# Top-k attention and a mixture of experts on one core: eight small routing operations per loop step for the first three batches, nine for the choices made on incomplete counts

## The chip, the core and the metric

The kernel runs on one core of a Trainium2 chip. The metric is the device time of one execution in microseconds (us), the median of several executions. Five engines work side by side, each through its own queue of instructions in program order: PE (TensorE, matmuls), DVE (VectorE), ACT (ScalarE), POOL (GpSimd) and SP (SyncE, which issues transfers here). They wait for each other through semaphores.

## What is computed

Inputs are q, k and v (8 batches, 8 heads, 576 positions, 64 columns), a modality per token, a gate of 8 experts and the experts' weights. Per head, every row of scores keeps its 32 largest values, and the softmax over them weighs v. The 4608 rows of 512 columns go to the expert with the largest logit:

```
scores = scale * np.matmul(q, k.transpose(0, 1, 3, 2))
kth = np.partition(scores, -top_k, axis=-1)[..., -top_k:-top_k + 1]
scores = np.where(scores >= kth, scores, -1000000000.0)
attn = softmax(scores)
x = np.matmul(attn, v), rows of all heads side by side
logits = x @ w_gate + modality_bias[modality_id]
e_idx = np.argmax(logits, axis=1)
out[e_idx == e] = gate_w * (np.maximum(x @ w1[e], 0.0) @ w2[e])
```

## The kernel before

**The attention loop.** The 32 pairs of heads are cut into 9 tiles of 128 rows each, 288 tiles in all, 36 to a batch. The loop over `i` takes one step per tile and works on many tiles at once, each at another stage. In step `i` PE makes the scores of tile i + 2 (L396), ACT copies them to `Ssb` (L404), and DVE finds the eight largest of each of seven pieces of tile i (`subs`, L411, "piece maxima"). For tile i - 1 DVE runs the selection chain (`chain`, L422 to L424: MAX8, MATCH_REPLACE8 and so on, each reading what the one before wrote). ACT makes `K` (L443), POOL the product `y` (L449), DVE the MAX8 over `y` (L453, `find`), every third step three operations that pick the threshold (`pick`, L460 to L462), ACT the exponential `ex` (L467), and DVE ends the step with `keep` (L473), which writes the masked probabilities `P`. POOL waits for `P` (`gate`, L477) before it makes the next `y`. PE transposes `P` (L488) and multiplies with v (L516).

**The order on DVE within a step.** It is written out by hand. List `a_` is the chain, `b_` the piece maxima and `find`, and `c_` the pick, the small operations of the step and `keep`. If `c_` holds more than `keep`, up to HOLD = 4 entries of `b_` are held back and put between the last entries of `c_`. `weave` spreads the rest of `b_` behind the entries of `a_`.

**Routing.** When a batch is done, `logits`, `logit_rows` and `xrow` bring its rows and logits into place, and `route` returns a list of small operations: bias, maximum, exponential (ACT, `r_ez`, L631), one-hot (L632 to L635), `ranks` (PE L607 to L611, ACT copy `r_rk`, L612), two products on POOL (L640, L641, put in `behind`, which is run at the step's end), the sum of the gate (L642 to L644), `total` (L616, which reads POOL's product), `dest` (L646), two token operations on POOL (L647, L648), and `count_up` (L649), which adds the batch to the experts' counts. The list goes into `side`. A `PAUSE` in it ends the step's share. Then five sends (`sendq`, POOL L620) scatter the rows to the buffer `xs`, one per step; POOL divides the rows by the softmax sums (L556), one or two halves a step.

**Slots.** A slot takes up to 256 rows of one expert. After each counted batch two more slots may be chosen (`more_moe`): `sched` makes the list of the choice (DVE L703 to L723, "choice"), the expert's number is loaded by SP (L727), then its weights (L751, L755) and, behind the sends, the gathered rows `xg` (L732), which `tokens` copies (L743 to L746). These go into `rush`. Slots below PB = 6 choose on counts that don't yet fill a slot for certain. PE's work of a slot (L784 to L825) is spread over the steps by `spare_pe`. Before the first slot starts, `keep_warm` (L931) gives PE six matmuls a step that nobody reads. Each step takes from `rush` up to RN = 6 operations and, when `rush` is empty, from `side` so many that the step has SN = 4:

```
for x in range(RN if rush else 0):
    ...
for x in range(SN - len(small_)):
```

**The tail.** Twelve slots run within the loop; the rest, seven here, run behind it one after another (`slot`, L1011 to L1034).

Of the kernel before, what the change touches and what calls it, by code (L numbers as in the profile page):

```python
# [26 lines left out]
SN = 4  # L27
# [23 lines left out]
PB = 6  # L51
COST = {"trans": 0.5, "qk": 0.5, "mix": 1.12, "rest": 0.22, "t": 0.11, "prep": 0.43, "logits": 1.2, "xrow": 0.54, "av": 0.42, "av8": 0.17}
RN = 6
QO = 0
EB = 3
RLF = (0, 1)
# [14 lines left out]
def kernel(  # L71
# [14 lines left out]
    B, H, S, D = q.shape  # L86
# [28 lines left out]
    PAUSE = lambda: None  # L115
# [284 lines left out]
    def sevac(i, parts=False):  # L400
        T[i]["S"] = sb = wk.tile([128, S], FT, name="Ssb", bufs=LR + 1 + QL - QO)
        sv = sb.rearrange("p (a b) -> p a b", a=2)
        for x in (slice(0, 1), slice(1, 2)) if parts else (slice(0, 2),):
            A.activation(sv[:, x], T[i]["ps"][:, x, :288], AF.Copy, scale=0.125)  # L404
# [188 lines left out]
    def route(lg, bias, oh, x5b, early=False):  # L593
# [24 lines left out]
        def send(c):  # L618
# [23 lines left out]
            lambda: V.tensor_reduce(sm, ez, axis=AX.X, op=OP.add),  # L642
            lambda: V.tensor_scalar(sm, sm, EPS, None, op0=OP.add),
            lambda: V.reciprocal(x5b[:, :, GW], sm),  # L644
            total,
            lambda: V.tensor_scalar(dest, ps5, float(ZROW), None, op0=OP.add),  # L646
            lambda: G.tensor_scalar(x5b[:, :, TOK], tokb, 1.0, 1.0, op0=OP.mult, op1=OP.mult),  # L647
# [210 lines left out]
    rush = deque()  # L858
# [3 lines left out]
    seen = [0]  # L862
    nslot = [0]
# [201 lines left out]
    for i in range(LAST):  # L1065
# [8 lines left out]
        def scores():  # L1074
            if ok(i + QL):
                pp, jj = divmod(i + QL, 9)
                qk(i + QL, pp, jj, qbd[pp % 2])

        if ok(i + QL):
            cost += COST["mix" if (i + QL) % 9 == 8 else "qk"]  # L1080
        if QO == 0:
            scores()
# [12 lines left out]
        while nxt:  # L1095
            nxt.popleft()()
        if ok(i + QL) and QO == 0:
            sevac(i + QL)
# [20 lines left out]
        if 0 <= b1 < B:  # L1119
            if r == 0:  # L1120
                chore.extend(recip(b1, den[b1 % 2]))
            rl, rx = (RLF, RXF) if b1 in (0, B - 1) else (RLM, RXM) if b1 < EB else (RL, RX)
            if r == rl[0]:
                rows_of[b1] = logits(b1, xTs(b1))
                cost += COST["logits"]
            if r == rl[1]:
                logit_rows(b1, rows_of[b1], lgb[b1 % 2], later if 0 < b1 < EB else late)
                cost += COST["xrow"]
            if r in rx:
                xrow(b1, rx.index(r), xTs(b1), x5)  # L1130
                cost += COST["xrow"]

            def done(n=b1 + 1):
                seen[0] = n * S
                fresh.clear()
            if r == rl[1] + (3 if 0 < b1 < EB else 2):
                steps, sends, count_up = route(lgb[b1 % 2], bias_all[:, b1], ohb[b1 % 2], x5, b1 < EB)
                side.extend(steps)
                if b1 < EB:
                    side.extend([count_up, done, lambda x=sends, n=5 * b1: sendq.extend((c, f, n + c) for c, f in enumerate(x))])  # L1140
            if b1 >= EB and r == max(rl[1], rx[4]) + 3:
                side.extend([f for x in sends for f in (x, PAUSE)] + [count_up, done])
# [8 lines left out]
        while seen[0] and spare_pe > 0:  # L1151
# [9 lines left out]
            spare_pe -= c  # L1161
        if QO == 1:
            scores()
# [13 lines left out]
        for x, f in enumerate(lo):  # L1177
            b_.insert(LOP[x] if x < len(LOP) else len(b_), f)
        small_ = []
        for x in range(RN if rush else 0):  # L1180
            if rush and rush[0] is WAIT and sendq:
                break
            f = rush.popleft() if rush else PAUSE
            if f is PAUSE:
                break
            small_.append(f)
        if not small_:
            while bulk and not PJ[1] < j <= PJ[2]:
                chore.append(bulk.popleft())
            while chore:  # L1190
                small_.append(chore.popleft())
        for x in range(SN - len(small_)):
            if side and side[0] in quiet and PJ[1] < j <= PJ[2]:
                break
            f = side.popleft() if side and not rush else PAUSE
            if f is PAUSE:
                break
            small_.append(f)
# [130 lines left out]
    def slow():  # L1329
# [6 lines left out]
        with tc.For_i(0, B, 1) as b:  # L1336
# [25 lines left out]
            for c in range(5):  # L1362
                xrow(0, c, xTs(0), x5)
                flush()
            steps, sends, count_up = route(lgb[0], sb[:, 0], ohb[0], x5)
            for f in (*steps, *sends, count_up):
                f()
# [39 lines left out]
```

## Time and profile before

| what | us |
|---|---|
| median of 3 executions (1254.93, 1257.7, 1256.58) | 1256.58 |
| the profiled execution, its own time | 1256.33 |
| its span, first to last instruction | 1254.5 |
| DVE busy | 1156.4 (92%), 5827 instructions |
| PE busy | 1182.1 (94%) |
| ACT busy | 1018.0 (81%) |
| POOL busy | 687.8 (55%) |
| granted TensorE clock, mean | 0.983 of full speed |

Busy times are sums over the span of one profiled execution; they say which engine has little room, and the views by stretch say where. An idle time is put down to the engine whose event ended it. A line such as L411 is a line of the kernel before.

### The profile page before, as it was taken

What the parts mean: (1) busy time and instruction counts of PE and PEld (TensorE: products, weight loads), DVE (VectorE), ACT (ScalarE), POOL (GpSimd) and SP (SyncE); (2) the same over time, 40 slices, a digit from 0 to 9 for tenths busy, and PEclk for the clock granted to TensorE, in tenths of its full rate; (3) what the DMA queues carried; (4) which work ended last, traced back from release to release, by engine and by line L of the source; (5) the groups of instructions that cost most, each with busy time, mean ns of one, the idle gap of its engine ahead of it and who ended that gap; (6) DMA issues with size and microseconds to landing.
All of it is one profiled execution on the core that took longest, in us unless ns stands there. A gap on an engine that the chain in (4) does not pass through costs nothing. (4 is left out here: it accounts for less than half of the span.)

```text
span 1254.5 us, 29230 instructions
## 1 busy us (share of the span) xinstructions
PE 1182.1 (94%) x8141; PEld 929.6 (74%) x8141; DVE 1156.4 (92%) x5827; ACT 1018.0 (81%) x2042; POOL 687.8 (55%) x1342
## 2 busy tenths in 40 slices
PE   7888888899999999999999999999999999899995
PEld 6666676776868677786867777787868766799894
DVE  5999999999999999999999999999999995866764
ACT  4899988889989998988988988898889885555553
POOL 3555558456765576656865676556766772511110
PEclk8899998999999999999999999999999999999998
DMA  6665334775477557565476466666586423777563
GB/s 132 161 177 124 87 87 130 189 195 156 92 204 211 135 151 198 164 170 137 128 219 175 121 186 192 183 158 165 135 240 162 125 93 101 232 242 269 196 217 124
DMA packets 210133, 205.80 MB, mean 164 GB/s; under 512 B 106365, under 2 KB 155517, under 8 KB 209952
## 3 DMA queue, kind: packets, MB, share of 16 engines
q1 hardware_dynamic: 202384, 183.61, 54.1%
q0 software_dynamic: 6208, 19.54, 4.4%
q8 instruction: 70, 1.15, 0.4%
q14 instruction: 111, 0.91, 0.2%
q10 hardware_dynamic: 1360, 0.59, 0.2%
HBM read 123.35 MB, written 24.23 MB: 118 GB/s over the span
## 5 line engine op out<-in xcount | busy, mean ns | idle before, releaser
L411 DVE MAX8 cand<-Ssb 128x8 f32<-128x82 f32 (+1 forms) x2016 | 430.8, 231 | 8.9 <-ACT Ssb L404 8.9
L449 POOL TENSOR_TENSOR y<-Ssb,K 128x576 f32<-128x576 f32 x288 | 366.8, 1274 | 4.7 <-ACT K L443 4.1
L396 PE MATMUL S<-ks,qs 128*128 128x288 f32 x1016 | 232.9, 352 | 34.4 <-ACT Ssb L404 25.0
L404 ACT ACTIVATE Ssb<-S 128x576 f32<-128x576 f32 (+1 forms) x289 | 189.2, 655 | 72.0 <-PE S L396 53.0
L443 ACT ACTIVATE K<-Ssb,n 128x576 bf16<-128x576 f32 x288 | 227.8, 791 | 13.0 <-POOL y L449 12.5
L396 PEld LDWEIGHTS S<-ks,qs 128*128 128x128 f32 x1016 | 158.1, 193 | 91.9 <-issue 39.7
L467 ACT ACTIVATE ex<-Ssb,sm 128x576 f32<-128x576 f32 x288 | 226.1, 785 | 0.0
L453 DVE MAX8 mg<-y 128x8 f32<-128x576 f32 x288 | 214.6, 745 | 2.1 <-POOL y L449 2.1
L473 DVE SCALAR_TENSOR_TENSOR P<-Ssb,kth,ex 128x576 f32<-128x576 f32 x256 | 213.7, 835 | 0.6 <-PE T L488 0.3
L496 ACT ACTIVATE PT<-T 128x640 f32<-128x640 f32 (+1 forms) x288 | 191.5, 665 | 8.1 <-PE T L488 8.1
L803 PE MATMUL E<-xgT,w1b 128*128 128x256 f32 x768 | 188.3, 387 | 4.6 <-ACT xgT L784 2.4
L815 PE MATMUL E<-w2b,hT 128*128 128x512 f32 x384 | 182.7, 600 | 0.7 <-ACT hT L807 0.3
L488 PE MATMUL T<-idf,P 128*128 128x128 f32 x1152 | 170.1, 275 | 0.0
L803 PEld LDWEIGHTS E<-xgT,w1b 128*128 128x128 f32 x768 | 139.3, 191 | 31.1 <-ACT xgT L784 3.9
L477 POOL TENSOR_SCALAR spare<-P 1x1 f32<-1x1 f32 x256 | 47.8, 187 | 207.9 <-DVE mg L422 191.1
L516 PE MATMUL X<-PT,vm 128*64 128x256 f32 (+1 forms) x1536 | 147.8, 335 | 3.5 <-ACT st L279 2.5
L488 PEld LDWEIGHTS T<-idf,P 128*128 128x128 f32 x1152 | 136.5, 141 | 3.5 <-issue 1.3
L436 POOL TENSOR_SCALAR n<-mg 128x1 f32<-128x1 f32 x288 | 65.9, 229 | 109.1 <-DVE mg L424 100.8
L516 PEld LDWEIGHTS X<-PT,vm 128*64 128x64 f32 x1536 | 85.8, 137 | 50.4 <-issue 16.6
L815 PEld LDWEIGHTS E<-w2b,hT 128*128 128x128 f32 x384 | 66.5, 190 | 54.2 <-issue 50.5
L556 POOL TENSOR_TENSOR x<-x,rd 128x256 f32<-128x256 f32 (+1 forms) x80 | 53.8, 678 | 27.8 <-ACT x L560 27.8
L443 ACT ACTIVATION_READ_ACCUMULATOR K<-Ssb,n 128x1 f32 x288 | 61.5, 213 | 0.0
(208 smaller groups left out, 2248.7 us busy)
## 6 DMA issues: line engine op xcount, KB each, us to landing
w1b<-in_moe_w_dram SPq DMA_DIRECT2D x80, 512.0 KB, 5.6
w2b<-in_moe_w_dram SPq DMA_DIRECT2D x80, 512.0 KB, 5.6
ks<-st SPq DMA_DIRECT2D x64, 288.0 KB, 3.7
qs<-st SPq DMA_DIRECT2D x126, 144.0 KB, 2.9
ks<-st SPq DMA_DIRECT2D x62, 256.0 KB, 5.0
xg<-xs SPq DMA_DIRECT2D x20, 516.0 KB, 3.8
vm<-in_v_dram SPq DMA_DIRECT2D x32, 256.0 KB, 3.2
km<-in_k_dram SPq DMA_DIRECT2D x63, 128.0 KB, 4.1
```

Source lines behind the costliest of these rows:

```text
L396: PE.matmul(ps[:, hf, u - a:v - a], l, d["ks"][:, x, h, u + o:v + o], start=(n == 0), stop=(n == len(terms) - 1), skip_group_check=(j == 8))
L411: return [lambda s=s: V.max(c[:, s * 8:s * 8 + 8], T[i]["S"][:, bnd[s]:bnd[s + 1]]) for s in range(NSUB)]
L443: A.activation(t["K"], t["S"], AF.Sign, scale=2.0 ** -24 - 1.0, bias=t["n"][:, 1, i % 3:i % 3 + 1], accum_out=t["n"][:, 0, i % 3:i % 3 + 1])
L449: G.tensor_tensor(t["y"], t["S"], t["K"], op=OP.mult)
L453: V.max(t["mg"][:, i % 3, 24:32], t["y"])
L467: A.activation(t["ex"], t["S"], AF.Exp, bias=t["s"][:, i % 3:i % 3 + 1])
L473: V.scalar_tensor_tensor(t["P"], t["S"], kth[:, i:i + 1], t["ex"], op0=OP.is_ge, op1=OP.mult, accum_out=dn)
L488: PE.transpose(T[i]["pt"][:, x, :], (Pm if c == 4 else Pb[c % 2])[:, h * 512 + x * 128:h * 512 + x * 128 + 128], idf)
L496: A.activation(o, T[i]["pt"][:, :n], AF.Copy)
L516: PE.matmul(o.rearrange("p (a b) -> p a b", a=2) if j < 8 else o, l, r, start=(c == 0), stop=(c == 4), skip_group_check=True)
L803: PE.matmul(ps[:, f % 2], w1b[:, c, f * 128:(f + 1) * 128], xgT[:, c, :], start=(c == 0), stop=(c == KC - 1))
L815: PE.matmul(o["py"], hT[:, f, t * 128:(t + 1) * 128], w2b[:, f, :], start=(f == 0), stop=(f == FC - 1))
```

## The change

Two numbers are added, SF = 8 and RF = 9, and a pause. Until the counts of three batches are complete (`seen[0] < EB * S`, EB = 3), a step takes from `side` up to SF instead of SN operations; while fewer than PB = 6 slots have begun, it takes from `rush` up to RF instead of RN. `total` reads a product that POOL makes at the end of a step, so in the routing of the first three batches (`early`) a PAUSE stands in front of it. Later batches and slots keep the old numbers.

```diff
@@ -51,6 +51,7 @@
 RN = 6
+SF, RF = 8, 9
 QO = 0
@@ -642,6 +643,7 @@
             lambda: V.reciprocal(x5b[:, :, GW], sm),
+            *[PAUSE] * early,
             total,
@@ -1177,7 +1179,7 @@
-        for x in range(RN if rush else 0):
+        for x in range((RN if nslot[0] >= PB else RF) if rush else 0):
             if rush and rush[0] is WAIT and sendq:
@@ -1189,7 +1191,7 @@
-        for x in range(SN - len(small_)):
+        for x in range((SN if seen[0] >= EB * S else SF) - len(small_)):
             if side and side[0] in quiet and PJ[1] < j <= PJ[2]:
```

Where instructions land is shown by the rows of the two programs' orders. In the changed kernel lines from L54 on are one higher, from L645 on two.

DVE, batch 0, kernel before: the step that begins with the reciprocal of the routing (`L644`) and ends with `keep`; `cand` and `Ssb` are the piece maxima, `dest` the rows' places:

```order
L644 RECIPROCAL x_186<-r_sm 128x5
L411 MAX cand<-Ssb 128x8
L616 TENSOR_REDUCE r_ps_3157<-r_pr 128x5
L411 MAX cand<-Ssb 128x8
L646 TENSOR_SCALAR dest<-r_ps_3157 128x5
L411 MAX cand<-Ssb 128x8 x2
L473 SCALAR_TENSOR_TENSOR P_154,den_162<-Ssb,kth,ex 128x576
```

The same place in the changed kernel; the reciprocal has moved to the step before, and the count (`L651`, L649 before) into this step, a step earlier than it stood:

```order
L617 TENSOR_REDUCE r_ps_3157<-r_pr 128x5
L648 TENSOR_SCALAR dest<-r_ps_3157 128x5
L412 MAX cand<-Ssb 128x8
L651 TENSOR_TENSOR tbl<-tbl,r_rk 128x8
L412 MAX cand<-Ssb 128x8 x3
L474 SCALAR_TENSOR_TENSOR P_153,den_162<-Ssb,kth,ex 128x576
```

The conversion to `dest` now stands directly behind the sum that it reads, and the three last piece maxima stand together.

DVE, the first choice after batch 0, kernel before, its first step (`tbl` holds the counts, `s_key` and `s_oh` the choice):

```order
L703 TENSOR_TENSOR tbl<-tbl 128x8
L713 SCALAR_TENSOR_TENSOR tbl<-tbl,eoff 128x8
L704 SCALAR_TENSOR_TENSOR s_key<-tbl,rev 128x8
L411 MAX cand<-Ssb 128x8
L714 TENSOR_TENSOR tbl<-tbl 128x8
L411 MAX cand<-Ssb 128x8
L705 MAX s_m_3585<-s_key 128x8
L411 MAX cand<-Ssb 128x8
L706 TENSOR_SCALAR s_oh<-s_key,s_m_3585 128x8
L411 MAX cand<-Ssb 128x8
L473 SCALAR_TENSOR_TENSOR P_153,den_162<-Ssb,kth,ex 128x576
```

And in the changed kernel, up to the ninth operation of the same step:

```order
L705 TENSOR_TENSOR tbl<-tbl 128x8
L715 SCALAR_TENSOR_TENSOR tbl<-tbl,eoff 128x8
L706 SCALAR_TENSOR_TENSOR s_key<-tbl,rev 128x8
L716 TENSOR_TENSOR tbl<-tbl 128x8
L707 MAX s_m_3462<-s_key 128x8
L708 TENSOR_SCALAR s_oh<-s_key,s_m_3462 128x8
L412 MAX cand<-Ssb 128x8
L702 TENSOR_TENSOR s_hit<-tbl,s_oh 128x40
L412 MAX cand<-Ssb 128x8
L703 TENSOR_REDUCE s_sc<-s_hit 128x5
L412 MAX cand<-Ssb 128x8
L719 TENSOR_SCALAR s_ft<-pos,s_sc 128x2
```

Six operations stand in a row where three stood, and three that belonged to the next step have come into this one.

SP, from the last of the four loads of the first expert's `w1b` to the first gathered rows, kernel before (the stacks `ks` and `qs` stand ahead of this piece; `km`, `qm` and `kqt` are loads for a coming pair of heads):

```order
L751 ISA
L751 DMA w1b<-in_moe_w_dram 128x4x256
L134 DMA km<-in_k_dram 128x4x64 x2
L140 DMA kqt<-in_k_dram 64x2x64
L134 DMA qm<-in_q_dram 128x4x64 x2
L140 DMA kqt<-in_q_dram 64x2x64
L731 TENSOR_LOAD sei_168
L731 ISA x2
L732 ISA
L732 DMA xg<-xs 128x1032
```

And in the changed kernel, the same piece; `km` follows right behind it:

```order
L753 ISA
L753 DMA w1b<-in_moe_w_dram 128x4x256
L317 DMA ks<-st 64x2x576 x2
L317 DMA ks<-st 64x2x512
L317 DMA ks<-st 64x2x64
L317 DMA ks<-st 64x2x512
L317 DMA ks<-st 64x2x64
L319 DMA qs<-st 64x576 x4
L733 TENSOR_LOAD sei_168
L733 ISA x2
L734 ISA
L734 DMA xg<-xs 128x1032
```

The weights have moved ahead of the stacks, and the gathered rows ahead of the loads of k and q.

## Rows read from the trace of the kernel before

**Rows 1.** Stretches: engine's busy us (instructions) PE, PEld, DVE, ACT, POOL; clock, DMA.

```profile
25.00:520.00 495.00, 459.15 (x3315) 354.73 (x3313) 491.20 (x2688) 438.36 (x898) 301.42 (x584) 0.98 0.59 155
520.00:1020.00 500.00, 491.74 (x3331) 376.73 (x3328) 496.43 (x2657) 446.33 (x926) 327.07 (x629) 1.00 0.61 164
1020.00:1254.50 234.50, 214.20 (x1391) 183.92 (x1389) 156.93 (x409) 126.35 (x206) 53.66 (x104) 0.98 0.56 186
```

**Rows 2.** Waits of DVE, 25 to 1020 us: us in total, times, longest.

```profile
DVE sgt L743 <- DMA xg<-xs: 1.2, 1, 1.2
DVE mg L453 <- POOL y L449: 1.0, 2, 0.8
```

**Rows 3.** Timeline of DVE, a chain's start in a step with small operations (start us, us).

```profile
195.93 0.21 DVE L422 MAX8 mg<-cand 128x8 f32<-128x56 f32 x1
...
196.25 0.20 DVE L422 MATCH_REPLACE8 cand<-mg,cand 128x56 f32<-128x56 f32 x1
```

**Rows 4.** Timeline of DVE, a chain's start in a step without them.

```profile
1019.64 0.22 DVE L422 MAX8 mg<-cand 128x8 f32<-128x56 f32 x1
1019.77 0.23 DVE L411 MAX8 cand<-Ssb 128x8 f32<-128x82 f32 x1
...
1019.98 0.20 DVE L422 MATCH_REPLACE8 cand<-mg,cand 128x56 f32<-128x56 f32 x1
1020.10 0.24 DVE L411 MAX8 cand<-Ssb 128x8 f32<-128x82 f32 x1
```

**Rows 5.** Timeline of DVE, small operations with and without a reader behind them.

```profile
206.32 0.18 DVE L700 TENSOR_TENSOR s_hit<-tbl,s_oh 128x40 f32<-128x40 f32 x1
206.54 0.20 DVE L701 TENSOR_REDUCE s_sc<-s_hit 128x5 f32<-128x40 f32 x1
...
1018.12 0.17 DVE L460 TENSOR_TENSOR eq<-i9s,n 128x27 f32<-128x27 f32 x1
1018.20 0.24 DVE L411 MAX8 cand<-Ssb 128x8 f32<-128x82 f32 x1
```

**Rows 6.** Timeline of SP's queue around the first gathered rows.

```profile
209.00 3.22 SPq L318 DMA_DIRECT2D qs<-st  x4
214.47 2.46 SPq L751 DMA_DIRECT2D w1b<-in_moe_w_dram  x4
217.04 2.01 SPq L134 DMA_DIRECT2D km<-in_k_dram  x2
...
223.18 1.10 SPq L140 DMA_DIRECT2D kqt<-in_q_dram  x1
225.14 0.37 SPq L732 DMA_DIRECT2D xg<-xs  x1
```

**Rows 7.** Waits of ACT, whole span: the copy of the ranks.

```profile
ACT r_rk L612 <- PE X L611: 7.0, 6, 1.7
```

**Rows 8.** Timeline of ACT, batch 1.

```profile
336.57 0.77 ACT L467 ACTIVATE ex<-Ssb,sm 128x576 f32<-128x576 f32 x1
```

**Rows 9.** Timeline of DVE, instructions that stretch, batches 1 and 2.

```profile
338.46 2.20 DVE L473 SCALAR_TENSOR_TENSOR P<-Ssb,kth,ex 128x576 f32<-128x576 f32 x1
...
455.00 0.67 DVE L460 TENSOR_TENSOR eq<-i9s,n 128x27 f32<-128x27 f32 x1
455.60 0.67 DVE L632 SCALAR_TENSOR_TENSOR r_key<-r_z,rev 128x40 f32<-128x40 f32 x1
456.19 0.64 DVE L461 TENSOR_TENSOR jk<-eq,mg 128x27 f32<-128x27 f32 x1
```

**Rows 10.** Timeline of POOL at the same places.

```profile
335.03 0.53 POOL L640 TENSOR_TENSOR r_pb<-r_rk,tbl 128x40 f32<-128x40 f32 x1 [0.79 <-ACT r_rk L612]
...
338.20 1.27 POOL L449 TENSOR_TENSOR y<-Ssb,K 128x576 f32<-128x576 f32 x1
...
454.35 1.28 POOL L449 TENSOR_TENSOR y<-Ssb,K 128x576 f32<-128x576 f32 x1
455.60 1.18 POOL L556 TENSOR_TENSOR x<-x,rd 128x256 f32<-128x256 f32 x2
```

## The prediction

> **What bounds the kernel now.** Read the stretches first [rows 1]: three pieces of the span, each with the busy time of every engine. From 25 to 1020 us, in both pieces of the attention loop, VectorE (DVE) is busy, 491.20 of 495 and 496.43 of 500 us, together 987.63 of 995. No other engine comes near that everywhere, and the end of this loop is the end of a queue of DVE instructions that nearly touch. Behind 1020 us the tail of seven expert slots runs, where DVE has gaps and PE sets the pace. Then read who made DVE wait in that loop [rows 2]: the longest entry is one wait of 1.2 us for the gathered rows `xg`; 1.0 us goes to two late products of POOL. So a change in this loop gains or loses only what changes (a) in DVE's idle time, 7.4 us in all, (b) in how tightly its instructions follow each other, and (c) in instructions that stretch. A wait that moves on another engine is worth nothing until it reaches DVE.
>
> DVE instructions overlap when the second doesn't read what the first writes, and (b) can be read off. In [rows 3] the first MAX8 of the selection chain starts at 195.93 and the MATCH_REPLACE8 that reads its result at 196.25: 0.32 us with nothing useful between. In [rows 4] an independent piece maximum (L411) starts 0.13 behind the same MAX8, and the replace comes at 1019.98, 0.34 behind: the piece maximum was nearly free. The small operations act alike [rows 5]: L701 reads what L700 wrote and starts 0.22 behind it; L460 is followed by an operation that doesn't need it after 0.08.
>
> **The change, part by part.** No arithmetic is added or removed. DVE, ACT, POOL and SP execute the same instructions in another order. PE loses 12 keep-warm matmuls, since the first expert slot begins two loop steps sooner; nobody reads them, and DVE hides them. From the count of the last batch to the end the order of all engines is the same, and the choices see the same counts as before, so the number of slots in the tail can't change.
>
> *Fewer loop steps with small operations.* Routing of batches 0, 1 and 2 takes two steps fewer, and each choice for the first slots also fewer. In a step that carries small operations the kernel holds four piece maxima back to mix with them, and then the selection chain has none to put behind its first MAX8. The order of the instructions has 105 places before and 98 after where MATCH_REPLACE8 stands directly behind its MAX8. Seven fewer, at 0.32 - 0.12 = 0.2 us each (0.12 is where the next instruction follows the replace at the end of [rows 4], and 0.13 behind the MAX8): **-1.4 us**. The far end is no gain, if the freed piece maximum must be paid for elsewhere; I take the row, since it is the same pair of instructions.
>
> *Denser small operations.* Eight or nine per step are more than the four held pieces can separate. In the new order three dest conversions stand directly behind the sum they read, three one-hot comparisons behind their MAX8, two mask operations and one key reduction likewise; three places of the kind vanish: net six more. At 0.22 - 0.08 = 0.14 us [rows 5], less where the reader is short, I take 0.12: **+0.7 us**, between 0 and 0.9.
>
> *The wait for `xg`.* SP issues transfers in order. Before [rows 6], it hands out the stacks `ks` and `qs` until 212.2, then the first expert's `w1b` from 214.47, then two loads each of k and q of a coming pair, and only at 225.14 `xg`; those loads stand between `w1b` and `xg` from 217.04 to 224.3. DVE copies from `xg` in the step around 227.4 and waits 1.2 us [rows 2]. In the new order the choice is made a step after the count and ends in the step after that, so `w1b` goes out ahead of the stacks; `xg` stands behind the stacks and ahead of the k and q loads. The five sends that `xg` must follow start two steps sooner, as does the copy that reads it, so this distance is unchanged; what is gone is some 7 us of other issues in front. That is more than the 1.2 us missing: **-1.2 us**. If the stacks wait long for their source it could stay (0) or, by the same size, double (+1.2); I take the gain, as the margin is six times the wait. The k and q loads that are now behind `xg` are for a pair whose scores are several steps off; PE, not DVE, would notice first, and [rows 2] has hardly an entry of DVE for that chain.
>
> *ACT and POOL queues.* The copy of the ranks (L612) now stands right behind the exponential of the routing in ACT's queue, where it waits for the one-hot from DVE and for PE. Such waits exist already: 7.0 us over six, 1.7 the longest [rows 7]. They are covered by the distance between ACT's `ex` and the P that reads it; at one of the tightest places, batch 1, `ex` ends at 337.34 [rows 8] and its P starts at 338.46 [rows 9], 1.1 us later. Six tenths more wait per batch fit there. Cost: 0; if the cover were gone, about 0.6 us in each of batches 1 and 2. The sends move too: the first two of each batch now fall into steps in which POOL also divides rows. POOL then finishes `y` later in the step, and this is the third kind of cost.
>
> *Instructions that stretch.* P of [rows 9] starts at 338.46 and takes 2.20 us; POOL's `y` [rows 10] runs from 338.20 to 339.47, so at least 1.0 us of it is standing still. At 455.00 three operations with two SBUF inputs take 0.67, 0.67 and 0.64 us [rows 9], each ending as a POOL operation of [rows 10] ends (the last of them as the pair of divisions from 455.60 does, 456.78), against 0.17 for L460 in [rows 5]: 1.5 us. The Trainium skill, SBUF — State Buffer, section Who interferes with whom, says that a DVE instruction with two SBUF inputs contends with a GpSimd instruction that reads SBUF, and that whichever issues first keeps the port while the other blocks entirely. These rows agree, and the rule speaks against this change: it packs choices, full of such operations, into steps where POOL still divides. Without the page: such pile-ups hit batches 1 and 2 today, and the new order makes some and dissolves some. The late `y` at 338.20 stands behind L640, which had waited 0.79 us for the ranks [rows 10]; those ranks are issued a step sooner in the new order. I take the sum of pile-ups as **0**, between -2.5 (the two shown vanish: 1.0 + 1.5) and +7.5 (each of three batches gets both anew).
>
> **Sum.** 1256.33 us of the profiled execution (span 1254.5 and 1.83 around it) - 1.4 + 0.7 - 1.2 + 0 = **1254.4 us**. The profiled execution stands 0.25 below the median 1256.58, so against the median this is -2.2 us or 0.17%; a measurement of this kernel tells about 0.2%, 2.5 us, from no change.
>
> **The rivals.**
> - *More comes back.* The pile-ups of [rows 9] don't recur, as the ranks arrive sooner and choices meet POOL's sends instead of its divisions: 1254.4 - 2.5 = 1251.9 us. For it: both events are accidents of timing in the very stretch that is rearranged. Against it: the divisions remain where they were, and the denser steps meet them.
> - *Slower by collisions.* Dense two-input operations and late `y` meet in the steps that now hold two divisions and a send: each batch pays 2.5 us anew, 1254.4 + 7.5 = 1261.9 us. It takes away the gain from the first 2.2 us on, and makes the kernel measurably slower from 4.7 us, two batches of 2.5. Against it: only five or six steps per batch are concerned, and in them DVE's own steps grow longer too, which gives POOL time. The page's rule above is this mechanism.
> - *It doesn't reach the end.* The freed places are refilled, the copy waits for `xg` as before: 1256.3 us. For it: the same DVE instructions must run, and 99% of the loop is already theirs.
>
> **How the numbers follow.** Forecast 0.38, more comes back 0.30, no effect 0.18, collisions 0.14. A quarter of the forecast's own case lies beyond -2.5 us, since it stands near that edge: faster 0.10 + 0.30 = 0.40. Slower: most of the collision case, 0.12. Within 0.2%: 0.48. The range takes in, below, both shown pile-ups and no cost of the dense operations, 1254.4 - 2.5 - 0.7 = 1251.2, and above, three piles of 1.5, 1254.4 + 4.5 = 1258.9; the rest of the collision case is left out.
>
> **What would show it.** DVE in the loop as busy as before; no entry for `xg` in DVE's waits; `xg` issued some 8 us sooner; in batch 1 no P over 2 us; the piece maximum between MAX8 and replace in seven more steps. The loop would end about 2 us sooner and the tail keep its length. Wrong would be: a new DVE wait for `ex` or `Ssb` in batch 1 or 2, two-input operations over 0.6 us in the choice's step, or a difference that arises behind 1020 us.

## The result and the profile after

The changed kernel took **1261.22 us** (median of 9, 1259.22 to 1264.38) beside 1255.55 us of the kernel before on the same chip: ratio 1.0051, interval 1.0037 to 1.0066. It is slower by 5.7 us, 0.5%. The forecast was 1254.4 us with a range that ended at 1258.9; the time lies outside it and close to the rival "slower by collisions", 1261.9.

The first view is the stretches of the profiled execution (span 1262.4), which answer to [rows 1]: busy us (instructions) of PE, PEld, DVE, ACT, POOL, then clock and DMA.

```profile
25.00:520.00 495.00, 455.14 (x3270) 352.22 (x3269) 490.63 (x2651) 433.76 (x892) 298.31 (x578) 0.98 0.58 153
520.00:1020.00 500.00, 490.72 (x3325) 374.99 (x3319) 497.32 (x2662) 443.63 (x924) 328.00 (x624) 1.00 0.61 163
1020.00:1262.40 242.40, 221.02 (x1427) 188.38 (x1426) 163.32 (x442) 131.61 (x216) 62.22 (x116) 0.97 0.54 185
```

DVE is as busy as before, 987.95 of 995 us (987.63 before), but gets through fewer instructions in that time: 2651 up to 520 us, where it did 2688. So DVE does not idle more; its instructions last longer or follow each other less tightly. The waits of DVE between 25 and 1020 us say the same, and answer to [rows 2] (the second lies at 27 us, ahead of anything that was changed):

```profile
DVE r_sm L643 <- ACT r_ez L632: 0.8, 1, 0.8
DVE cand L412 <- ACT Ssb L405: 0.7, 1, 0.7
DVE sgt L745 <- DMA xg<-xs: 0.4, 2, 0.2
```

The long wait for `xg` is down from 1.2 us to 0.4 us in all, nearly as forecast, since SP hands `xg` out ahead of the k and q loads. The timeline of SP's queue, to set beside [rows 6]:

```profile
202.90 2.98 SPq L753 DMA_DIRECT2D w1b<-in_moe_w_dram  x4
...
212.45 5.90 SPq L319 DMA_DIRECT2D qs<-st  x4
219.37 0.35 SPq L734 DMA_DIRECT2D xg<-xs  x1
219.82 1.28 SPq L135 DMA_DIRECT2D km<-in_k_dram  x2
```

Which instructions last longer is seen in the groups by form (the list of instruction groups, 25 to 1020 us; count, then busy us and mean ns). First the kernel before, then the changed one:

```profile
L706 DVE TENSOR_SCALAR s_oh<-s_key,s_m 128x8 f32<-128x8 f32 x12 | 2.8, 233 | 0.0
L717 DVE TENSOR_SCALAR s_ft<-pos,s_sc 128x2 f32<-128x2 f32 x6 | 2.1, 346 | 0.1
L718 DVE TENSOR_SCALAR smk<-pos,s_sc 128x2 f32<-128x2 f32 x6 | 1.6, 272 | 0.0
L460 DVE TENSOR_TENSOR eq<-i9s,n 128x27 f32<-128x27 f32 x93 | 23.3, 250 | 0.0
```

```profile
L708 DVE TENSOR_SCALAR s_oh<-s_key,s_m 128x8 f32<-128x8 f32 x12 | 3.8, 316 | 0.1
L719 DVE TENSOR_SCALAR s_ft<-pos,s_sc 128x2 f32<-128x2 f32 x6 | 3.0, 502 | 0.1
L720 DVE TENSOR_SCALAR smk<-pos,s_sc 128x2 f32<-128x2 f32 x6 | 2.5, 416 | 0.0
L461 DVE TENSOR_TENSOR eq<-i9s,n 128x27 f32<-128x27 f32 x92 | 24.4, 265 | 0.0
```

The same operations of 8, 2 and 27 columns cost 0.9 to 1.1 us more per group. Each group grows by single events. Here are three such operations, with one `P` between them, on DVE's timeline (start us, us):

```profile
336.16 1.18 DVE L651 TENSOR_TENSOR tbl<-tbl,r_rk 128x8 f32<-128x8 f32 x1
...
337.71 0.79 DVE L474 SCALAR_TENSOR_TENSOR P<-Ssb,kth,ex 128x576 f32<-128x576 f32 x1
...
341.27 1.42 DVE L708 TENSOR_SCALAR s_oh<-s_key,s_m 128x8 f32<-128x8 f32 x1
...
473.56 1.61 DVE L719 TENSOR_SCALAR s_ft<-pos,s_sc 128x2 f32<-128x2 f32 x1
```

And POOL's timeline at these places, with what stands ahead of the `y` in each:

```profile
336.04 1.27 POOL L450 TENSOR_TENSOR y<-Ssb,K 128x576 f32<-128x576 f32 x1
337.28 1.70 POOL L557 TENSOR_TENSOR x<-x,rd 128x256 f32<-128x256 f32 x2
339.14 1.06 POOL L621 DMA_INDIRECT xs<-x,dest  x1 [0.16 <-DVE cand L412]
...
340.80 0.47 POOL L323 TENSOR_SCALAR qbd<-qs 128x64 fp32r<-128x64 f32 x2
...
341.38 1.27 POOL L450 TENSOR_TENSOR y<-Ssb,K 128x576 f32<-128x576 f32 x1
...
471.19 1.07 POOL L621 DMA_INDIRECT xs<-x,dest  x1 [0.16 <-DVE cand L424]
...
473.28 1.28 POOL L450 TENSOR_TENSOR y<-Ssb,K 128x576 f32<-128x576 f32 x1
474.53 0.61 POOL L557 TENSOR_TENSOR x<-x,rd 64x256 f32<-64x256 f32 x1
```

The operation at 336.16 ends as a `y` does (337.34 and 337.31). The one at 341.27 should take 0.2 us; it ends at 342.69, as `y` ends (342.65). The one at 473.56 lasts through a `y` and the division behind it (475.17 and 475.14). It works the other way too: the two divisions at 337.28, beside which `P` ran, took 1.70 us, where such a pair takes 1.18 us [rows 10]. In the step before 341.38 POOL did a `y`, two divisions, a send (L621) and two copies for `qbd` before it came to the next `y`, which so began in the middle of DVE's choice and not beside its selection chain. Three windows, from one end of P to the next, show how full POOL got (columns as in the stretches). They are one step each of batches 0, 1 and 2, in which the changed kernel loses 1.4, 1.0 and 1.5 us; first these steps in the kernel before, then in the changed one.

```profile
192.08:196.01 3.93, 3.93 (x50) 3.58 (x49) 3.90 (x22) 3.43 (x8) 3.69 (x8) 1.00 0.00 0
335.44:340.66 5.22, 4.83 (x30) 4.10 (x27) 5.18 (x25) 5.22 (x12) 4.91 (x12) 1.00 0.94 205
465.88:470.39 4.51, 4.51 (x33) 3.10 (x33) 4.48 (x26) 4.51 (x10) 3.20 (x10) 1.00 0.70 170
```

```profile
193.42:198.77 5.35, 3.81 (x46) 3.21 (x43) 5.28 (x28) 3.43 (x8) 4.21 (x10) 1.00 0.22 86
338.50:344.75 6.25, 6.25 (x42) 4.74 (x41) 6.18 (x32) 5.68 (x13) 5.66 (x12) 1.00 0.94 234
469.98:476.03 6.05, 5.88 (x39) 4.75 (x41) 5.98 (x31) 6.05 (x13) 5.54 (x11) 1.00 0.93 227
```

POOL's part (the last busy number) rises from 3.69, 4.91 and 3.20 us to 4.21, 5.66 and 5.54 us. Most steps around them last 3.1 to 4.4 us, so in batches 1 and 2 POOL has more to do than fits into such a step. Not all of the growth is loss: DVE's instructions in the three steps rise from 22, 25 and 26 to 28, 32 and 31, and some of the steps behind get shorter by 0.7 to 1.0 us, as they have given work away.

**A ledger.** To compare many kernels I split DVE's time from the end of the first P to the end of the last in three. For each form of instruction the lower quartile of its durations is its usual one; what a single instruction takes over that, from 0.12 us on, is *stretched* time; idle time with a releaser is *wait*; the rest is *pace*. Before: pace 979.9, wait 5.4, stretched 30.9 us. Changed: 981.0, 4.8 and 36.1: **+1.1, -0.6, +5.2**, together 5.7 us. From 25 to 1025 us, 9.3 us in 15 instructions ended with a `y` before, 17.3 us in 26 after; divisions stood behind 10.2 and 11.7 us, and the rest was 8.7 and 4.4. All of the growth lies before 520 us.

A ledger is worth no more than its one profiled execution. The two executions here took 1256.33 and 1264.18 us, 7.9 us apart; beside the 5.7 us of the loop 0.4 us lie ahead of the first P and 1.7 us behind the last, where both kernels have the same order. That the loop's 5.7 us equal the difference of the medians is chance: for the variants below a ledger's sum misses the difference of the medians by up to 3.8 us. Entries move by about half a us with the way in which forms are grouped, and by up to 1.1 us between two executions of one kernel (section 6).

### The profile page after: what moved, and what is told of

Read it like the earlier page. It is cut to its first block, busy times and chain, and to the rows that moved or that the text cites. A ratio compares the mean times of both kernels' runs of the same rounds, so it can differ in the third digit from the quotient of the medians.

```text
span 1262.4 us, 29206 instructions
## 1 busy us (share of the span) xinstructions
PE 1184.2 (94%) x8129; PEld 930.2 (74%) x8129; DVE 1162.9 (92%) x5827; ACT 1015.7 (80%) x2042; POOL 694.2 (55%) x1342
```

## The experiments

The theories in the texts on record: COLLISIONS (or POOL FULL, SEND, DENSE for single parts of it), that DVE's small operations stand while a POOL instruction runs; RANKS, that ACT stands for the ranks and makes others late; MORE WAITS, that what is saved comes back as waits; ROOM, ORDER, ACT FULL and others are told where they come up. Differences in us are to the kernel before of the same comparison, whose median lay between 1254.2 and 1256.4 us. "Ledger" gives pace, wait, stretched against the kernel before.

**1. Either half of the change alone.**

```diff
-SF, RF = 8, 9
+SF, RF = 8, 6        (sf_only, with the pause)
+SF, RF = 4, 9        (rf_only, without the pause)
```

> Routing of three batches eight per step with its pause, choices six per step as before. Theory 1 (DVE and POOL exclude each other where dense small operations, sends and divisions of rows share a step): the sends and the count already fall into the steps with divisions, so most of the loss is here, 2 to 5 us slower than before, and instructions of DVE over 1 us stand in the three routing stretches. Theory 2 (the dense choices alone cost, by their own order): within 1 us of before. Theory 3 (the loss arises behind batch 2, by a shift of the later steps): within 2 us of before at the end of batch 2, the rest later.

> Choices nine per step, routing four per step without the added pause, as before. Theory 1: the choices start where they started before, behind the divisions, so at most 1 us slower, and faster by up to 1 us where the wait for the gathered rows goes. Theory 2: the larger part of the loss is here, 3 to 6 us slower. Theory 3: any value within 3 us, and the difference arises behind 520 us.

sf_only: 1268.07 us, ratio 1.0100 (1.0077 to 1.0123), worse than the whole change. Its waits of DVE begin so:

```profile
DVE sgt L745 <- DMA xg<-xs: 6.2, 1, 6.2
DVE lt L588 <- PE X L580: 1.5, 1, 1.5
```

rf_only: 1258.82 us, ratio 1.0038 (1.0021 to 1.0055). Its profiled execution was one of its quickest (1255.23), so its profile doesn't show the loss. Both are slower than the first theory on record had it (2 to 5 us, and at most 1). What follows: dense routing is the costlier half, and the dense choice mends what dense routing alone spoils, where DVE waits 6.2 us for `xg` (0.4 us in the whole change). The parts don't add up.

**2. Without the divisions**, in both kernels. The rows of x are not divided by their sums.

```diff
-            divide.extend([lambda a=a: half(a) for a in range(0, HP, 2)])
+            divide.extend([PAUSE for a in range(0, HP, 2)])
```

> The kernel before, with the division of the rows by the softmax sums on POOL left out (80 POOL instructions fewer; rows go to the experts undivided). Theory 1: DVE's stretched instructions in the routing of each batch shrink, 4 to 10 us faster than before over eight batches. Theories 2 and 3: POOL is no bound, within 2 us of before.

> The changed kernel with the same divisions left out. Theory 1: without POOL's divisions in the dense steps the loss against the kernel before with the same left out is gone, between 2 us faster and 1.5 us slower than that. Theory 2: 4 to 6 us slower than that one, as with divisions. Theory 3: 4 to 6 us slower, and the difference arises behind 520 us.

Before without divisions 1245.38 us (ratio 0.9918, 0.9902 to 0.9935), changed without them 1253.88 us (0.9989, 0.9973 to 1.0004). Without them the kernel before gains 9.6 us, yet the change still loses, 8.5 us. So the divisions alone are not its cause. The ledgers of the two stand at -0.3, +7.6, -13.1 and +1.1, +10.8, -11.5: of the 6.2 us between the two loops, stretching is 1.6 us where it was 5.2; waits are 3.2 and pace 1.4. Waits took its place. The waits of the changed kernel without divisions:

```profile
DVE lt L588 <- PE X L580: 4.3, 3, 2.2
DVE sgt L745 <- DMA xg<-xs: 4.0, 3, 1.8
DVE r_sm L643 <- ACT r_ez L632: 2.5, 2, 2.0
```

The kernel before without divisions has no wait for `r_ez`. My reading, which no run here tests, is that DVE, less hindered, comes to the sum over `r_ez` before ACT has made it. The expectation fell: this pair loses more than any theory allowed, and mostly by other means than stretching.

**3. Where POOL's work lies.** Four edits of the changed kernel: sends two steps later (hold2), ranks one step later (rkp1), choice two steps later (pick_late), one division in place of two in steps with five small operations or more (div_small1).

```diff
+        if sendq and i >= held_to[-1] and rows_made[0] > sendq[0][2] ...   (hold2)
+            *[PAUSE] * (RKP + early),                                      (rkp1)
+            rush.extend([PAUSE] * (2 if n < PB else 0) + pick + [begin] ...  (pick_late)
+        for _ in range(min(len(divide), 2 if len(divide) > 2 and len(small_) < 5 else 1)):  (div_small1)
```

> The changed kernel, with the sends of the routed rows (POOL L621) held back two loop steps for the first three batches, so that they start about where they did before. The changed kernel took 1261.22 us. Theory SEND (sends now fall into steps in which POOL still divides rows and DVE runs a choice; POOL gets behind, and its product y then stands across a small operation of DVE): the small operations at 211.72, 341.27, 473.56 and 477.92 lose their 1.2 + 1.2 + 1.3 + 0.9 us, so about 1256.6 us, between 1255 and 1258.5. Theory RANKS (ACT stands for the ranks directly behind the exponential of the routing, and y and P get late by that): the sends don't matter, 1261 us, within 1.5. Theory DENSE (many small operations in one step collide with whatever POOL does): 1261 us as well.

> The changed kernel, with the matrix products of the ranks and their copy (L612, L613) one loop step later than the one-hot comparison for the first three batches. Theory RANKS: ACT's waits for the ranks (1.8 us in batch 0, 0.8 in batch 2), DVE's wait for r_ez (0.8) and the late POOL product r_pb (2.3 us of waiting in batch 2) go, and with them the stretched count at 336.16 (1.0) and the stretched P at 468.37 (0.8): 0.8 + 1.0 + 0.8 = 2.6 us, 1258.6 us. Theory SEND: sends start one step later, which dissolves some of the four collisions with a send: 1259 to 1261 us, with the r_ez wait gone but the stretched choice operations there. Theory DENSE: 1261 us, within 1.5.

> The changed kernel, with two empty loop steps ahead of each choice for a slot of the first three batches; routing and sends stay where they are. Theory SEND: the choices now meet fewer of the steps with a send; the stretched choice operations (1.2 at 341.27, 1.3 at 473.56, 0.9 at 477.92, 0.9 at 195.3) go, 1257 us, unless the later steps hold a send too, then 1259. Theory RANKS: nothing moves ahead of the count, 1261 us. Theory DENSE: the same density, 1261 us. Price in any case: the rows xg come two steps later, and a wait for them of up to 1.2 us as before may come back.

> The changed kernel, where POOL divides half as many rows (one instruction in place of two) in a loop step that holds five small operations or more; what is left over comes in later steps, and a send that waits for its rows comes later with it. Theory SEND, as a matter of POOL's load per step: POOL has 0.6 us less in each of the full steps, y starts earlier there: 2 to 4 us back, 1257 to 1259 us. Theory DENSE with the divisions as what is met: the stretched operations at 190.81, 195.31 and 195.86 (1.1 + 0.5 + 0.4) go, 1259 us. Theory RANKS: 1261 us.

| kernel | us | ratio, interval | ledger |
|---|---|---|---|
| hold2 | 1258.30 | 1.0028, 1.0015 to 1.0041 | +1.0, -1.4, +2.5 |
| rkp1 | 1263.11 | 1.0071, 1.0052 to 1.0089 | +1.7, +3.2, +2.7 |
| pick_late | 1265.89 | 1.0094, 1.0074 to 1.0114 | +0.5, +2.1, +7.1 |
| div_small1 | 1260.15 | 1.0047, 1.0030 to 1.0063 | +1.7, +2.5, +2.0 |

hold2 does what SEND said, at the upper end of its range: half of the stretching goes, and 3 us with it. Three of the four events that it named (341.27, 473.56, 477.92) are gone, the one at 211.72 stayed (1.34 us in that run); a dest conversion of 2.36 us and a P of 2.77 us are new. RANKS is right on its events and wrong on the time: with the ranks later the wait for `r_ez` is gone, and so are the long operation at 336.16 and a long P at 468.37, but in their place two P of batches 1 and 2 last 2.34 and 2.35 us, `xg` comes late (3.7 us, once), and the kernel is slower. So late ranks have a share in the stretching, and moving them doesn't pay. pick_late went against every theory: its stretched time rose, though the same sends meet fewer choices. Its trace shows the longest of them in the steps of the routing, which the edit doesn't move: two dest conversions of 1.24 and 1.80 us and a P of 2.78 us; of the choices, two first operations (L705) meet a `y`, 1.06 and 0.93 us. Why the routing meets POOL at other moments I did not settle. div_small1 takes 3.2 us of stretching away and gives 3.1 us back as waits for `xg` (1.4) and `y` (1.8) and others: MORE WAITS, as the rival had it.

**4. Both reliefs, and the other direction.** hold2_div joins hold2 and div_small1. before_div spreads the divisions in the kernel before (from three small operations on; in one late batch the last rows go out with one half undivided). pool_dense and pool_sparse add POOL work that nobody reads, in 21 crowded steps of the changed kernel and in 21 of the kernel before (every second one of those with three small operations or more). The edit of the first:

```diff
+        if i < 160 and len(small_) > 4:
+            for _ in range(4):
+                G.tensor_tensor(dummy, idf, idf, op=OP.mult)
```

> The changed kernel with both reliefs of POOL together: the sends held back two loop steps (alone 1258.3 us), and half as many divisions in a step with five small operations or more (alone 1260.15 us). In the trace of the first, the largest stretched operation left was the conversion of dest (L648), 3.0 us more than before, each standing until a division ends. Theory COLLISIONS (the loss of the change is DVE's small operations standing while POOL's y and divisions run): the dest conversions go back to about 0.2 us, 3 us are gained on the first, 1255.3 us, and DVE's stretched time falls below that of the kernel before (28.2 us in the loop). Rival MORE WAITS (what is taken from collisions comes back as waits for y, xg and r_ez, as it did where only the divisions were spread): 1258 us, within 1.5.

> The kernel before, with half as many divisions in a loop step that holds three small operations or more. Theory COLLISIONS: in the kernel before, 10.2 us of DVE's stretched time end with a division; in the first three batches that is 4.8 us, and half of it would go: 1252.5 us against 1255. Rival MORE WAITS: the rows are sent later, xg comes later, DVE waits for it 2 to 4 us more: 1255 to 1258 us.

> The changed kernel, with four more products of 128x128 on POOL (some 1.2 us together, nobody reads them) at the end of each of the 21 loop steps of the first 160 that hold five small operations or more. Theory COLLISIONS: in these steps POOL has no room left, y of the next step gets late by the whole addition and stands across DVE's small operations or P, 0.7 to 1.2 us per step: 15 to 25 us more than the 1261.2 us of the changed kernel. Rival ROOM (POOL, busy for two thirds of the loop, has room in these steps; what costs is order and waits): under 5 us more. The pair run is the kernel before with the same addition in 21 of its steps.

> The kernel before, with the same four products on POOL at the end of 21 loop steps, every second one of the 42 that hold three small operations or more. Theory COLLISIONS: with four small operations per step fewer of them meet a late y, and every second step lets POOL catch up: 0.3 to 0.6 us per step, 6 to 12 us more than 1255 us, at most half of what the pair run pays. Rival ROOM: under 5 us more, and as much as in the pair run.

hold2_div: 1257.91 us, ratio 1.0006 (0.9993 to 1.0019), ledger +2.1, +1.3, -1.0. before_div: 1256.29 us, ratio 1.0000 (0.9985 to 1.0015): nothing to be had there. pool_dense: 1282.34 us, 1.0203 (1.0180 to 1.0226). pool_sparse: 1271.98 us, 1.0118 (1.0096 to 1.0141).

In hold2_div the three steps look like this (windows as above), with POOL busy for about half of each:

```profile
192.05:196.62 4.57, 4.57 (x56) 4.11 (x54) 4.50 (x29) 3.72 (x9) 2.20 (x4) 1.00 0.00 0
337.62:342.46 4.84, 4.84 (x34) 3.87 (x34) 4.77 (x31) 4.84 (x10) 2.38 (x5) 1.00 0.91 206
468.67:473.51 4.84, 4.84 (x34) 3.89 (x34) 4.77 (x31) 4.84 (x10) 2.38 (x5) 1.00 0.91 206
```

The longest of them fell from 6.25 to 4.84 us, though the step ahead of it in batches 1 and 2 is now 5.29 us long (section 6). The added products of the other pair took 0.47 us each on average (84 of them, half of them 0.40 or less), 1.9 us per step and not the 1.2 of the text. The changed kernel stood 25.9 us above the kernel before with them, 20.2 more than the 5.7 of the change: 1.0 per step. The kernel before paid 15.5 us, 0.7 per step. So half of the added time reaches the end in the one and two fifths in the other: POOL has little room in these steps in either kernel, and the rival ROOM fell. The forecast for pool_sparse, at most half of the pair, fell too: density makes it worse, but the kernel before is near the edge itself. The kernel before paid by stretching: its stretched time rose by 15 us and its waits by 1. This is the plainest evidence here that POOL's work alone, with the same order on DVE, makes DVE's instructions last longer. The changed kernel paid by this line of DVE's waits, with only 2 us more stretching:

```profile
DVE mg L454 <- POOL y L450: 17.2, 11, 3.0
```

**5. Less POOL work, the same order.** ACT divides half of each row as it copies it, POOL the other half:

```diff
-            A.activation(x5b[:n_, c, :Dm]..., ps[:n_], AF.Copy)
+            A.activation(x5b[:n_, c, :256]..., ps[:n_, 0:2], AF.Copy)
+            for a in range(2, HP):
+                for h in range(2):
+                    A.activation(x[:, a, h], ps[:n_, a, h * 64:h * 64 + 64], AF.Copy, scale=RD[u][...])
-            divide.extend([lambda a=a: half(a) for a in range(0, HP, 2)])
+            divide.append(lambda: half(0))
```

A step then takes at most one division, and a send waits for one division of its rows in place of two.

> The kernel before, where ACT divides half of each row as it evacuates it (a copy of 256 columns and four scaled copies of 64 in place of one copy of 512), and POOL only the other half: POOL loses 20 of its 40 divisions, about 12 us of work; the order of DVE is the same. Theory POOL FULL (in the steps with small operations POOL's queue sets the pace): half of the 9.6 us that leaving all divisions out gave, about 1251 us. Rival ACT FULL (ACT is busy for 27.2 of the 29 us from 447 to 476, and takes on about 0.5 us per row): the 10 us on ACT reach the end in part, 1255 to 1260 us.

> The changed kernel with the same edit of the division. Theory POOL FULL: the change's loss shrinks with POOL's load, from 5.7 us to 3 or less against the run before_half; about 1254 us. Rival ORDER (the loss hangs on which instructions meet, not on how much POOL has to do): the same 5 to 6 us above the run before_half. ACT FULL would lift both alike.

> The changed kernel with the sends held back two loop steps, and the same edit of the division: a kernel with both reliefs of POOL. Theory POOL FULL: level with the run before_half or up to 2 us below it, 1249 to 1251 us, as the predicted gains (no wait for xg, a piece maximum behind the first MAX8) are then left over. Rival ORDER: 2 to 4 us above before_half, as the run hold2 against the kernel before. ACT FULL: 1255 us or more.

(The trace has 80 divisions, not 40, so POOL lost 40 of them.) before_half 1256.46 us (1.0011, 1.0001 to 1.0021), after_half 1259.31 us (1.0029, 1.0017 to 1.0040), hold2_half 1258.11 us (1.0018, 1.0007 to 1.0029). By the medians the change's loss is 2.9 us here, half of 5.7, which speaks for POOL FULL against ORDER. The profiles don't bear it out: the loops of the two profiled executions are 5.9 us apart (pace +1.4, waits +1.6, stretched +2.9), so stretching is nearly halved, and waits and pace make up for it. hold2_half stands 1.7 us above before_half, between what the two theories gave. The level did not fall to 1251 us: before_half has 4.8 us less stretched time but 5.9 us more waits, for logits from PE, `xg` and `ex`. Relieving POOL at ACT's cost won nothing here.

**6. What is left.** hold2_div_tok moves POOL's two token copies out of the step of the dest conversion; rkp1_div joins the later ranks and the spread divisions; hold2_div ran once more.

```diff
         return [
+            lambda: G.tensor_scalar(x5b[:, :, TOK], tokb, ...),
+            lambda: G.tensor_scalar(tokb, tokb, ...),
             lambda: V.tensor_tensor(l2, lg, bias, op=OP.add),
```

> The kernel with both reliefs (sends two steps later, divisions spread; ratio 1.0006 to the kernel before), with POOL's two token copies (L649, L650) moved from the step of the dest conversion to the start of the routing. In the trace of the kernel with both reliefs the dest conversion still stands 1.78 us in batches 1 and 2 (at 334.43 and 465.49), through a late y (334.33) and the division behind it; the token copies stand right ahead of this y and take 0.5 us. Theory COLLISIONS: y starts 0.5 us sooner there, the dest conversion is caught by the rest of it alone, and 0.5 to 1.2 us per batch come back: ratio 0.999, between 0.998 and 1.000. Rival MORE WAITS: what is left of the loss are waits (lt 1.5, y 1.8 us), and the ratio stays at 1.0006 or rises.

> The changed kernel with the ranks one step later than the one-hot comparison (alone: ratio 1.0071) and half as many divisions in the steps with five small operations or more (alone: 1.0047); the sends aren't held. Theory POOL FULL: the stretched time falls as it did with the divisions spread (by 3 us), ratio 1.005 or below. Rival WAITS: later ranks make the rows xg late (DVE waited 3.7 us for them in the run with the ranks alone), spread divisions make the sends and xg later still, and the ratio is 1.007 or more.

> The kernel with the sends held back two steps and the divisions spread, once more beside new runs of the kernel before, whose own median stood at 1256.44 us in the first of the two comparisons and between 1254.2 and 1255.8 us in most others. Reading A (both reliefs take away the whole loss): ratio 1.000 to 1.001 again. Reading B (they take away about half, and the first ratio leaned on a slow kernel before): the kernel itself at 1257.9 us again, ratio 1.002 to 1.003, as in the run with the token copies moved.

hold2_div_tok: 1257.61 us, 1.0026 (1.0013 to 1.0039), ledger +2.2, +0.7, -1.0. rkp1_div: 1260.54 us, 1.0038 (1.0025 to 1.0050), ledger +1.8, +1.8, +3.0. hold2_div again: 1257.71 us, 1.0022 (1.0009 to 1.0034), ledger +1.9, +1.8, -2.1. The event that the first was to cure is this, in hold2_div, on DVE and on POOL (in the second execution it took 1.43 us in batch 1 and 1.20 in batch 2, not 1.78):

```profile
334.22 0.18 DVE L617 TENSOR_REDUCE r_ps<-r_pr 128x5 f32<-128x40 f32 x1
334.43 1.78 DVE L648 TENSOR_SCALAR dest<-r_ps 128x5 int32<-128x5 f32 x1
```

```profile
331.86 0.60 POOL L641 TENSOR_TENSOR r_pb<-r_rk,tbl 128x40 f32<-128x40 f32 x1 [1.51 <-ACT r_rk L613]
...
334.33 1.27 POOL L450 TENSOR_TENSOR y<-Ssb,K 128x576 f32<-128x576 f32 x1
335.58 0.60 POOL L557 TENSOR_TENSOR x<-x,rd 128x256 f32<-128x256 f32 x1
```

With the token copies gone the conversion took 0.18 and 0.74 us in batches 1 and 2, and the time did not move: the forecast of 0.999 fell. Reading B holds: both reliefs bring the kernel to 1257.7 to 1257.9 us, and some 2 to 3 us of the loss stay although the stretched time is below that of the kernel before. What stays stands in the ledger as pace, +1.9 to +2.2, and waits, +0.7 to +1.8, for logits, `y` and `r_ez`. No run here takes the denser order alone away, so what makes this pace is argued, not shown. No kernel here beat the kernel before with its work complete.

## Why the prediction was wrong

**The step that failed** is "I take the sum of pile-ups as 0". It measured +5.2 us in the ledger, between the ends that the text gave, -2.5 and +7.5, and nearer to the dear one. Taking 6.2 us of stretching away (hold2_div) gave 3.3 us of time back (1261.22 to 1257.91), so not all of the 5.2 is loss by itself. Its ground, that the new order makes some pile-ups and dissolves some, is half true: the P at 338.46 [rows 9] is back at its usual length, and of the three operations at 455.00 one, L632, is still long (0.66 us); but some steps later, at 468.37, a P lasts 1.61 us. Yet the text had itself seen that the first two sends of each batch fall into steps in which POOL also divides, and did not add that step up. From [rows 10] it would have been a `y` of 1.27, two divisions of 1.18 together and a send (1.06 in the trace above), 3.5 us of POOL, and with the five short operations around them (1.1 us from 340.21 to 341.41) more than the 3.1 to 4.4 us of a step. A queue that is longer than its step hands its lateness on, and the next `y` starts where DVE's small operations stand. POOL's 55% of the span hid this. A second source was in the forecast's sight and priced at nothing as well: POOL waits for the ranks (2.31 us ahead of L641 in batch 2 of the changed kernel, 0.87 us in batch 1), and `y` is late by that.

**The rival "slower by collisions"** had the mechanism, its place and nearly the time, 1261.9 for 1261.22. The time is luck: its pile-ups are 2.3 us dearer than the 5.2 measured, and the other terms that it shares with the forecast are 2.4 us too cheap (-1.9 where +0.5 was measured). It was given 0.14 for two reasons. One was that only five or six steps per batch are concerned; that is enough. The other was that DVE's steps grow and give POOL time; they grew in part because POOL held DVE up. Its price per batch, 2.5 us, was higher than the 1.1 that the stretches 180 to 230, 318 to 360 and 450 to 495 us paid on average (1.3, 1.2 and 0.9; 1.1 more came at 506.36, where a `y` late behind the write of an expert's rows, L832, caught the threshold's comparison, 1.29 us), and it took operations with two inputs alone to be at risk.

**The other terms.** *Fewer steps* (-1.4): DVE's pace at L422 fell by 1.0 us; right in sign, a little small. *Denser operations* (+0.7, at most 0.9): pace as a whole rose by 1.1, so with the -1.0 out of it the dense order costs 2.1 us; in it the sum, the maximum, the one-hot and the masks (L616, L705, L706, L717, L718) each took 0.3 to 0.4 us more than in the kernel before. The bound of 0.9, from one pair of rows, was too low. *The wait for `xg`* (-1.2): it fell from 1.2 to 0.4, -0.8. *ACT's queue* (0): a new wait of 0.8 for `r_ez` in batch 2, where the text had named `ex` and `Ssb` as signs of error, and the copy of the ranks waited 11.0 us in 8 places where [rows 7] had 7.0 in 6. The sum of these without the pile-ups, +1.1 - 0.6 = +0.5, would have been "no change", not the -1.9 of the forecast.

**The Trainium skill**, SBUF — State Buffer, section Who interferes with whom, says that copies, casts and tensor_scalar operations can, where their operands meet the conditions, enter modes with two ports and then contend with GpSimd too, and that tensor_reduce on this chip never does. The trace agrees: of the operations in the changed kernel's loop that start beside a `y` or a division with at least 0.35 us to go, all 5 of the kinds TENSOR_SCALAR and COPY lasted 0.35 to 1.33 us longer than usual, and none of the 5 TENSOR_REDUCE, 101 MATCH_REPLACE8 and 916 MAX8 lasted more than 0.02 us longer. So which operations are at risk can be told from their kind. The prediction used the same section for two inputs only, and so counted too few operations at risk.

## What to carry to other kernels

Before small operations are packed more densely, add up every engine's queue for each step that gets shorter or fuller, with its transfers, and not only the queue of the engine that bounds the kernel: an engine that is busy for half of the span can have more to do than fits into just these steps. Where two engines hold each other up, an off-path engine that is late by one instruction can cost the bound engine nearly that instruction's whole length (1.2 us of a `y` of 1.27 at 341.27). And cure a collision only after looking at what waits behind it: of the stretching cured, nearly all came back as waits in div_small1 (3.1 of 3.2 us), and half of it as waits and pace in hold2_div (2.9 of 6.2).

## What the runs showed that was not expected

- DVE operations of 2 to 8 columns, usually 0.15 to 0.3 us long, lasted up to 1.78 us in hold2_div, through two POOL instructions in a row (`y` to 335.60, a division to 336.18; the dest conversion 334.43 to 336.21).
- Leaving out 80 divisions of 53.8 us together gained 9.6 us on a kernel in which POOL is busy for 55% of the span; moving half of that work to ACT gained nothing.
- The kernel before itself came out at medians from 1254.2 to 1256.4 us in six comparisons of 17 to 29 runs, so that one ratio of a variant read 1.0006 and the next 1.0022; the second comparison was needed to read it.
